# Three whole heads and a pad of eight in each block of 128 features

## The chip, the cores and the metric

The kernel runs on one core of a Trainium2 chip. Its time is device microseconds of one execution; the kernel before takes 280.08 us, the median of three runs (280.01 to 280.14). The engines are named as the profile names them: PE is TensorE (PEld its weight loads), DVE is VectorE, ACT is ScalarE, POOL is GpSimd, SP is the engine that issues nearly all DMAs.

## The reference

A transformer block with linear attention over 2048 positions of width 640, 32 heads of 20, and a gated feed-forward of width 1536. All inputs are bf16.

```python
def _A_ref(x, wqkv, w_phi, wo):
    B, S, D = x.shape
    H = 32; Dh = D // H
    qkv = (lambda x, *d: x.transpose(*d))((x @ wqkv).reshape(B, S, 3, H, Dh), 2, 0, 3, 1, 4)
    q, k, v = qkv[0], qkv[1], qkv[2]
    pq = jnp.einsum("bhsd,hdf->bhsf", q, w_phi)
    pk = jnp.einsum("bhsd,hdf->bhsf", k, w_phi)
    phi_q = jnp.concatenate([_softmax(pq, axis=-1), _softmax(-pq, axis=-1)], axis=-1)
    phi_k = jnp.concatenate([_softmax(pk, axis=-1), _softmax(-pk, axis=-1)], axis=-1)
    kv = jnp.einsum("bhsf,bhsd->bhfd", phi_k, v)
    z  = jnp.einsum("bhsf->bhf", phi_k)
    num = jnp.einsum("bhqf,bhfd->bhqd", phi_q, kv)
    den = jnp.einsum("bhqf,bhf->bhq", phi_q, z)[..., None] + 1e-6
    o = num / den
    return (lambda x, *d: x.transpose(*d))(o, 0, 2, 1, 3).reshape(B, S, D) @ wo

h = x + _A_ref(_layernorm(x), A_wqkv, A_w_phi, A_wo)
h2 = h + ((n @ w_gate) * (n @ w_up)) @ w_down      # n = _layernorm(h)
```

Each head has 40 features: the softmax of 20 scores and the softmax of the same scores negated. The 32 heads make 1280 features.

## The kernel before, in words

The positions are 16 tiles of 128, in four batches of four. The weights of the scores are folded once (`w_phi` into `wqkv`), so that a tile's scores are one projection of 640 columns. Work is cut into named units, each with instructions on several engines:

- `k`t, `v`t, `q`t (`keys`, `values`, `queries`): the projection of tile t on PE, ten matmuls of 320 columns (five blocks of the width by two halves, one half to each bank of a PSUM pair). For keys and queries DVE takes the largest score of the row (L818) and scales it (L821), and ACT writes two exponentials (L825), of the scores and of their negatives, in place side by side per head.
- `K`t: DVE adds up each of the 64 groups of 20 (L836) and takes the reciprocals (L838), POOL multiplies the features by them (L839). `Q`t: DVE adds up the groups (L858), and POOL scales the second half of each head against the first (L864, L869), since numerator and denominator share the rest. Then SP issues two DMA transposes (L471) of 640 features each, which bring the queries' features onto partitions.
- `A`t (`kv_mm`): for the key tiles t and t+1, K^T V. The 1280 features are ten blocks of 128 (`NQ`). A block starts and ends inside a head, so it touches four heads (`SL`), and its matmul streams the values of four heads and their column of ones: 4 x 21 = 84 columns (`KVW`). The features are the weights, the values the moving operand. Two units per pair of tiles, five blocks each, accumulate in the two banks of one PSUM pair that is held from the first A unit to `Aout`.
- `Aout` (`kv_out`): DVE brings K^T V to SBUF, multiplied by a mask (`Gk`) that keeps only a feature's own head (L905), and the column of sums likewise (L908), for each bank.
- `n`t (`num`): phi_q KV of tile t, ten matmuls of 84 columns; neighbouring blocks add into the head that they share. DVE divides (L939, L941). The result is turned (by SP, or by PE for tiles 0 and 1).
- `h`t (`watt`): the output projection, the residual and the sums of the second norm. `f`b.ft.j (`fu`): gate and up of one block of 128 hidden features for a batch, `d`t and `e`t (`fd`): down and the output.

All matmuls go through one helper, so they stand at L570, and are told apart by their tiles: `ps<-vaug,phik` with 84 columns is the A units, `ps<-KVsb,phiqT` the n units, `ps<-Wp,xT` the projections.

The order of the units on each engine is written out by hand in `ORDER` (L58 to L107): each engine runs its list strictly in that order. `Prog.place` assigns the buffers along those lists, among them the four PSUM pairs (`p_ps`) that all units share and the three buffers of query features (`p_eq`), and waits on semaphores follow from the reads and writes that each unit names.

Of the kernel before, what the change touches and what calls it, by code (L numbers as in the profile page):

```python
# [11 lines left out]
P = 128  # L12
# [18 lines left out]
NQ = 2 * NC  # L31
HQ = [P * c // DF for c in range(NQ)]
SL = 4
KVW = SL * E21

# [37 lines left out]
    "DVE":  # L73
# [12 lines left out]
    "ACT":  # L86
# [291 lines left out]
def _build(ctx, nc, A_x, A_wqkv, A_w_phi, A_wo, B_w_gate, B_w_up, B_w_down, out):  # L378
# [68 lines left out]
    p_ps, p_eq, p_ob, p_outb, p_t32, p_gate, p_junk = Pool(4), Pool(3), Pool(2), Pool(2), Pool(2), Pool(2), Pool(2)  # L447
# [13 lines left out]
    R_const, R_xone, R_tab = Reg(), Reg(), Reg()  # L461
# [86 lines left out]
    for a in range(NC):
        lo, hi = CH[a]
        n = hi - lo + 1  # L550

        def phi_op(e, a=a, lo=lo, hi=hi, n=n):
            return e.tensor_tensor(out=Phi[:, a, 0:DH * n].rearrange("p (h f) -> p h f", f=DH),
                                   in0=Wrows[:, a, :].unsqueeze(1).to_broadcast([P, n, DH]),
                                   in1=G[:, a, lo:hi + 1].unsqueeze(2).to_broadcast([P, n, DH]), op=ALU.mult)
# [260 lines left out]
    def softexp(v, t, i, dst, regs_, use=()):
        mx = lambda: PS[v.i][:, 1, MXC:MXC + 1]
        g.op("DVE", lambda e: e.tensor_reduce(out=mx(), in_=PS[v.i][:, :, 0:HALF], axis=AX.XY, op=ALU.max,  # L818
# [4 lines left out]
        for s in range(2):  # L823
            sc = rs if s == 0 else nrs
            g.op("ACT", lambda e, s=s, sc=sc: e.activation(  # L825
                out=signed(dst(), s), in_=PS[v.i][:, :, 0:HALF].rearrange("p b (h f) -> p b h f", f=DH), func=ACT.Exp,
                bias=nb[:, i:i + 1], scale=sc[:, t:t + 1]), rd=v.R + [R_nb[i], R_rs[t], R_nrs[t]], wr=[regs_[s]], use=[v] + list(use),
                t=0.775, lat=0.92)
# [287 lines left out]
```

## Time and profile before

| what | value |
|---|---|
| median of the runs | 280.08 us (280.01 to 280.14) |
| profiled execution, first to last instruction | 278.3 us (no other time of it is listed) |
| PE busy | 274.1 us, 99% |
| DVE busy | 165.3 us, 59% |
| ACT busy | 134.5 us, 48% |
| POOL busy | 106.2 us, 38% |
| 84-column matmuls of the A units | 160, busy 6.7 us |
| 84-column matmuls of the n units | 160, busy 8.7 us |

The page gives busy time over the whole span and, in 40 slices of some 7 us each, in tenths. "Idle before" in a group is time in which the engine stood still ahead of that group, with what ended most of it. A matmul's listed duration has its way through the array in it and overlaps the next one's; what a matmul costs in a row of matmuls is the distance from start to start, which the timeline's stretches give: (length less one listed duration) / (count less one).

### The profile page before, as it was taken

The page shows a single profiled execution, that of the slowest core. Times are in us where ns is not written, and L with a number is a line of the kernel's source. Part 1 is how long each engine was busy: PE and PEld are TensorE (multiplying, and loading weights), DVE is VectorE, ACT ScalarE, POOL GpSimd, SP SyncE. Part 2 cuts the span into 40 slices and gives each one's busy share as a digit, 9 for nine tenths or more (in the row PEclk, how much of TensorE's full clock was granted, in tenths as well). Part 3 has the DMA queues.
Part 4 walks back from the last instruction along what each step waited for, and adds up shares of the span by engine and source line. Part 5 has one row for each costly group of instructions (what it writes and reads, how often), then busy time and mean ns, then how long its engine had stood idle before and what let it go on. Part 6 is the DMA issues. An engine that isn't in the chain of part 4 may idle for free.

```text
span 278.3 us, 5485 instructions
## 1 busy us (share of the span) xinstructions
PE 274.1 (99%) x2239; PEld 186.9 (67%) x2239; DVE 165.3 (59%) x314; ACT 134.5 (48%) x229; POOL 106.2 (38%) x150
## 2 busy tenths in 40 slices
PE   8999999999999999999999999999999999999995
PEld 8877777777878888877656555776464444447773
DVE  1999999999999876588545845313251222324011
ACT  3478999899666465421764413113244314340132
POOL 5438889899732240061320903142100000250252
PEclk9999999999999999999999999999999999999999
DMA  7988886008864617969643031544312000000112
GB/s 196 277 148 185 126 271 251 0 2 236 167 82 110 97 27 155 336 100 198 88 111 82 24 71 27 123 89 97 94 30 20 0 0 2 0 24 24 49 47 71
DMA packets 65193, 28.06 MB, mean 101 GB/s; under 512 B 55697, under 2 KB 63889, under 8 KB 65169
## 3 DMA queue, kind: packets, MB, share of 16 engines
q1 hardware_dynamic: 64240, 27.37, 43.8%
q10 hardware_dynamic: 928, 0.35, 0.5%
q8 instruction: 17, 0.28, 0.4%
q14 instruction: 8, 0.06, 0.1%
HBM read 11.82 MB, written 2.62 MB: 52 GB/s over the span
## 4 chain that ended last, share of the span: by engine, by line
PE 95%; DMA 2%; SPq 1%; DVE 1%; issue 0%
PE ps L570 95%; DMA Wp<-in_A_wqkv_dram 2%; SPq L471 1%; PE ps L482 0%; DVE outb L1022 0%; SPq L467 0%; DVE KVsb L905 0%; DVE KVsb L908 0%; DVE nb L821 0%
## 5 line engine op out<-in xcount | busy, mean ns | idle before, releaser
L570 PE MATMUL ps<-phik,Wgu 128*128 128x512 bf16 (+1 forms) x600 | 107.5, 336 | 0.0
L570 PEld LDWEIGHTS ps<-phik,Wgu 128*128 128x128 bf16 x600 | 58.2, 98 | 43.6 <-DVE phik L981 1.8
L570 PE MATMUL ps<-Wp,xT 128*128 128x320 bf16 x480 | 69.0, 299 | 0.0
L981 DVE TENSOR_TENSOR phik<-ps,gate 128x512 bf16<-128x512 f32 (+1 forms) x60 | 33.9, 577 | 55.3 <-PE ps L570 50.1
L570 PE MATMUL ps<-vaug,phik 128*128 128x320 bf16 (+3 forms) x544 | 60.0, 270 | 0.0
L979 ACT ACTIVATE gate<-ps 128x512 bf16<-128x512 f32 (+1 forms) x60 | 29.8, 510 | 59.7 <-PE ps L570 40.8
L570 PEld LDWEIGHTS ps<-Wp,xT 128*128 128x128 bf16 x480 | 45.9, 98 | 17.6 <-DVE phik L981 0.2
L570 PEld LDWEIGHTS ps<-vaug,phik 128*128 128x128 bf16 x544 | 43.7, 97 | 15.7
L839 POOL TENSOR_TENSOR phik<-phik,Rk 128x1280 bf16<-128x1280 bf16 x16 | 37.5, 2356 | 5.1 <-DVE Rk L838 4.8
L997 POOL TENSOR_TENSOR outb<-t,x_all 128x640 bf16<-128x640 f32 x12 | 16.8, 1397 | 56.9 <-ACT t L994 49.6
L994 ACT ACTIVATE t<-ps,mh,rs 128x640 f32<-128x640 f32 x12 | 10.6, 882 | 37.1 <-PE ps L570 37.1
L818 DVE TENSOR_REDUCE ps<-ps 128x1 f32<-128x640 f32 x32 | 26.3, 824 | 1.6 <-PE ps L570 1.2
L858 DVE TENSOR_REDUCE Sq<-eq 128x64 f32<-128x1280 bf16 x16 | 23.5, 1471 | 3.5 <-ACT eq L825 3.5
L825 ACT ACTIVATE eq<-ps,nb,rs 128x640 bf16<-128x640 f32 x16 | 14.2, 885 | 20.3 <-DVE nb L821 11.7
L836 DVE TENSOR_REDUCE Ssum<-phik 128x64 f32<-128x1280 bf16 x16 | 23.5, 1474 | 0.0
L964 POOL TENSOR_SCALAR vpe<-shc 128x1 f32<-128x1 f32 x16 | 3.0, 190 | 52.7 <-ACT junk L563 51.7
L869 POOL TENSOR_TENSOR eq<-eq,rq 128x640 bf16<-128x640 bf16 x16 | 20.2, 1270 | 0.5
L864 POOL TENSOR_TENSOR rq<-Sq,rq 128x32 f32<-128x32 f32 x16 | 4.0, 254 | 41.5 <-DVE rq L863 41.5
L563 ACT ACTIVATE junk<-x_all 128x640 bf16<-128x640 bf16 x20 | 14.6, 732 | 4.4 <-DVE x_all L958 4.4
L825 ACT ACTIVATE phik<-ps,nb,rs 128x640 bf16<-128x640 f32 x16 | 14.2, 889 | 2.4 <-DVE nb L821 2.4
L825 ACT ACTIVATE phik<-ps,nb,nrs 128x640 bf16<-128x640 f32 x16 | 14.3, 894 | 0.0
L825 ACT ACTIVATE eq<-ps,nb,nrs 128x640 bf16<-128x640 f32 x16 | 14.2, 885 | 0.0
(86 smaller groups left out, 235.8 us busy)
## 6 DMA issues: line engine op xcount, KB each, us to landing
x_all<-in_A_x_dram SPq DMA_DIRECT2D x4, 640.0 KB, 5.2
out_dram<-outb SPq DMA_DIRECT2D x15, 160.0 KB, 1.8
Wgu<-in_B_w_gate_dram SPq DMA_DIRECT2D x1, 1920.0 KB, 11.1
Wgu<-in_B_w_up_dram SPq DMA_DIRECT2D x1, 1920.0 KB, 9.1
vaug<-in_B_w_down_dram SPq DMA_DIRECT2D x1, 1920.0 KB, 8.3
Wp<-in_A_wqkv_dram SPq DMA_DIRECT2D x1, 800.0 KB, 4.9
phiqT<-in_A_wqkv_dram SPq DMA_DIRECT2D x1, 800.0 KB, 6.5
Wo<-in_A_wo_dram SPq DMA_DIRECT2D x1, 800.0 KB, 6.8
```

The source lines that it names most:

```text
L563: g.op("ACT", lambda e: e.activation(out=junk[:, v.i, :], in_=in_, func=func, accum_out=acc), rd=rd, wr=wr, use=[v], t=0.73, lat=0.97)
L570: ins = e.matmul(o_, lhsT=l_, rhs=r_, start=s_, stop=p_, skip_group_check=True)
L818: g.op("DVE", lambda e: e.tensor_reduce(out=mx(), in_=PS[v.i][:, :, 0:HALF], axis=AX.XY, op=ALU.max, apply_absolute_value=True, negate=Tru ...
L825: g.op("ACT", lambda e, s=s, sc=sc: e.activation(out=signed(dst(), s), in_=PS[v.i][:, :, 0:HALF].rearrange("p b (h f) -> p b h f", f=DH), ...
L836: g.op("DVE", lambda e: e.tensor_reduce(out=Ssum[:, vs.i, :], in_=x, axis=AX.X, op=ALU.add), rd=R_phik[t], wr=vs.R, use=[vs], t=1.39, lat=1.5)
L839: g.op("POOL", lambda e: e.tensor_tensor(out=x, in0=x, in1=Rk[:, vr.i, :].unsqueeze(2).to_broadcast([P, 2 * H, DH]), op=ALU.mult), rd=vr.R ...
L858: g.op("DVE", lambda e: e.tensor_reduce(out=Sq[:, vs.i, :], in_=eq[:, b.i, :].rearrange("p (g f) -> p g f", f=DH), axis=AX.X, op=ALU.add), ...
L869: return e.tensor_tensor(out=x, in0=x, in1=rq[:, vr.i, :].unsqueeze(2).to_broadcast([P, H, DH]), op=ALU.mult)
L979: g.op("ACT", lambda e: e.activation(out=gate[:, vg.i, 0:P * n], in_=PS[v.i][:, 0, 0:P * n], func=ACT.Copy), rd=[v.R[0]], wr=vg.R, use=[v, ...
L981: g.op("DVE", lambda e: e.tensor_tensor(out=hhT[:, hb, ft, sl], in0=PS[v.i][:, 1, 0:P * n], in1=gate[:, vg.i, 0:P * n], op=ALU.mult), rd=[ ...
L994: g.op("ACT", lambda e: e.activation(out=t32[:, v3.i, :].rearrange("p (b n) -> p b n", b=2), in_=PS[v.i][:, :, 0:HALF], func=ACT.Identity, ...
L997: g.op("POOL", lambda e: e.tensor_tensor(out=outb[:, vo.i, :], in0=t32[:, v3.i, :], in1=x_all[:, t, :], op=ALU.add), rd=v3.R + [R_h[t]], w ...
```

## The change

A block of 128 features now holds exactly three heads (`HW`), 120 features, and a pad of eight in front (`PADW`). There are 11 blocks (`NQ`), the last with two heads and an empty slot. A block touches three heads, so the matmuls of the A and n units stream 63 columns; the last block's in the n units 42.

- The key features keep their dense layout behind a pad of eight zeros at the very front. A block of weights begins eight features ahead of its first head, so its pad rows are the last features of the head before. The mask `Gk` sets their rows of K^T V to zero. The last block begins one head early.
- The query features get the padded layout: `eq` has 1408 columns instead of 1280. The pads and the empty slot are set once to one (unit `pad` on POOL). Each of a query's two exponentials is written by two ACT instructions, one for ten blocks (600 scores) and one for the last (40). To let the first read run on across the two PSUM banks, the query projection now puts 300 columns at the end of the first bank and 340 at the start of the second, in matmuls of these widths. The sums, reciprocals and products run over 66 groups instead of 64.
- The transposes take five and six blocks instead of five and five; the blocks are split 5 and 6 (15 and 17 heads) in K^T V, its eviction and the n units too.
- `KVsb` lies where `Phi` was; the scratch of the sums of squares (`junk`) has one buffer instead of two.
- `ORDER` is new for all engines behind the first loads. Up to the first n unit each engine but POOL and ACT has the same units as before in its list. SP issues the second feed-forward weight (`lu`) directly behind the first (`lg`), ahead of the transposes of queries 0 and 1.

```diff
+HW = 3
+NQ = 11
+PADW = P - HW * DF
+KVW = HW * E21
+WB = ((0, 5), (5, NQ))
+HB = 5 * HW
...
 ORDER = {
     "PE":
...
-        "k12 v9 v12 v15 v14 k14 k15 A0 A2 A4 v8 q2 q3 A6 v10 A0 A2 A8 q5 A10 A4 A12 A6 A8 A10 A14 A12 A14 n1 n0 n0 n1 q7 "
+        "v14 k14 v12 k15 A0 A2 A0 q2 A2 A4 A4 q3 A6 v10 A6 q5 A8 A10 A8 A12 A10 A12 A14 A14 n0 n1 n0 n1 q7 n1 q4 n0 h1 h0 n2 q6 "
...
     "SP":
-        "in in in in in in in lwq t4 lT7 lT4 t2 lT5 lT6 t3 t1 t0 lx3 lT10 lT15 lT9 lT11 lT8 lT13 lT14 lT12 lx0 lwo lg Q0 "
-        "Q0 lu Q1 Q1 Q2 Q2 Q3 Q3 Q5 Q5 n2 n3 Q7 Q7 h2 Q4 h3 Q4 Q6 Q6 Q8 ld n7 n5 lx1 n4 n6 Q8 Q9 h5 lx2 Q9 h4 n8 h7 h6 "
+        "in in in in in in in lwq t4 lT7 lT4 t2 lT5 lT6 t3 t1 t0 lx3 lT10 lT15 lT9 lT11 lT8 lT13 lT14 lT12 lx0 lwo lg lu Q1 Q0 "
+        "Q1 Q0 Q2 Q2 Q3 Q3 Q5 Q5 n2 n3 Q7 Q7 h2 h3 Q4 Q4 ld Q6 n5 Q6 n7 lx1 Q8 n4 Q8 lx2 n6 n8 h7 Q9 Q9 h5 h6 h4 Q10 Q10 Q12 "
...
-    BK = sb([P, 2 * NT * D], BF16, "phik")
+    BK = sb([P, PADW + 2 * NT * D], BF16, "phik")
-    eq = sb([P, 3, 2 * D], BF16, "eq")
-    junk = sb([P, 2, D], BF16, "junk")
+    eq = sb([P, 3, NQ * P], BF16, "eq")
+    junk = sb([P, 1, D], BF16, "junk")
...
+    U("pad")
+    pool_op(lambda e: e.memset(eq[:, :, :].rearrange("p b (w n) -> p b w n", n=P)[:, :, :, 0:PADW], 1.0), 0.4, wr=[R_pad])
+    pool_op(lambda e: e.memset(eq[:, :, (NQ - 1) * P + PADW:(NQ - 1) * P + PADW + DF], 1.0), 0.2, app=[R_pad])
+    pool_op(lambda e: e.memset(BK[:, 0:PADW], 0.0), 0.1, wr=[R_pad0])
...
         for s in range(2):
             sc = rs if s == 0 else nrs
-            g.op("ACT", lambda e, s=s, sc=sc: e.activation(
-                out=signed(dst(), s), in_=PS[v.i][:, :, 0:HALF].rearrange("p b (h f) -> p b h f", f=DH), func=ACT.Exp,
...
+            for k, (to, of, n) in enumerate(pieces):
+                g.op("ACT", lambda e, s=s, sc=sc, to=to, of=of: e.activation(
+                    out=to(s), in_=of(), func=ACT.Exp, bias=nb[:, i:i + 1], scale=sc[:, t:t + 1]),
...
     def queries(t, after=()):
         U("q%d" % t)
-        v = proj(t, 0, after)
+        v = Buf(p_ps, 2)
+        cut = HB * DH
+        g.op("PE", lambda e: mms(e, [(flat(v)[:, 512 - cut:512] if bk == 0 else flat(v)[:, 512:512 + D - cut], xT[:, t, c, 0:P],
+                                      Wp[:, c, cut * bk:cut + (D - cut) * bk], c == 0, c == NC - 1)
+                                     for c in range(NC) for bk in range(2)]),
...
+        softexp(v, t, NT + t, lambda: score(0, D),
+                [(lambda s: feat()[:, 0:NQ - 1, :].rearrange("p w (h s f) -> p s w h f", s=2, f=DH)[:, s],
+                  lambda: score(0, 2 * cut).rearrange("p (w h f) -> p w h f", h=HW, f=DH), 2 * cut),
+                 (lambda s: feat()[:, NQ - 1, DF:].rearrange("p (h s f) -> p s h f", s=2, f=DH)[:, s],
+                  lambda: score(2 * cut, D).rearrange("p (h f) -> p h f", f=DH), D - 2 * cut)], b.R, [b])
...
-        for k in range(2):
-            transpose(lambda k=k: phiqT[:, bb, NC * k:NC * (k + 1), P * tt:P * (tt + 1)], lambda k=k: eq[:, b.i, D * k:D * (k + 1)],
+        for k, (w0, w1) in enumerate(WB):
+            transpose(lambda w0=w0, w1=w1: phiqT[:, bb, w0:w1, P * tt:P * (tt + 1)], lambda w0=w0, w1=w1: eq[:, b.i, P * w0:P * w1],
...
     def kv_mm(t0, t1):
...
-                for c in range(NC * k, NC * (k + 1)):
-                    lo = HQ[c]
-                    col = KVW * (c - NC * k)
+                for w in range(w0, w1):
+                    h0 = min(HW * w, H - HW)
                     for t in range(t0, t1):
-                        o_ = (t * H + lo) * E21
-                        lst.append((PS[v.i][:, k, col:col + KVW], phik[:, t, P * c:P * (c + 1)], BV[:, o_:o_ + KVW], first, False))
+                        k0, o_ = 2 * D * t + HW * DF * w, (t * H + h0) * E21
+                        if w == NQ - 1:
+                            k0 -= DF
+                        lst.append((PS[v.i][:, k, KVW * (w - w0):KVW * (w - w0 + 1)], BK[:, k0:k0 + P], BV[:, o_:o_ + KVW], first, False))
...
     def num(t):
...
+                for bk in range(b0, b1):
+                    for w in range(*WB[bk]):
+                        k0 = KVW * w + (E21 if w == NQ - 1 else 0)
+                        o_ = base + KVW * w
+                        n = KVW * (w + 1) - k0
+                        lst.append((flat(v)[:, o_:o_ + n], phiqT[:, bb, w, P * tt:P * (tt + 1)], KVsb[:, k0:k0 + n], w == WB[bk][0], False))
```

More of the change, by code (lines that the diff above doesn't have):

```diff
@@ L30 @@
 DF = 2 * DH
[L31 to L34, printed above, removed]
+HW = 3
[4 more added lines that the diff above has]
+HB = 5 * HW
 WOW = D + 4
@@ L425, in _build @@
     Rk = sb([P, 2, 2 * H], FP32, "Rk")
-    Sq = sb([P, 2, 2 * H], FP32, "Sq")
-    rq = sb([P, 2, H], FP32, "rq")
+    Sq = sb([P, 2, 2 * HW * NQ], FP32, "Sq")
+    rq = sb([P, 2, HW * NQ], FP32, "rq")
     rden = sb([P, 2, H], FP32, "rden")
-    phik = BK[:, :].rearrange("p (t n) -> p t n", t=NT)
+    Phi = PK[:, :].rearrange("p (a n) -> p a n", a=NC)
+    KVsb = PK[:, 0:NQ * KVW]
+    phik = BK[:, PADW:PADW + 2 * NT * D].rearrange("p (t n) -> p t n", t=NT)
     pq = phiqT[:, :, :, :].rearrange("p b c n -> p (b c n)")
@@ L851, in queries, with score, feat @@
         U("q%d" % t)
-        v = proj(t, 0, after)
+        v = Buf(p_ps, 2)
[3 more added lines that the diff above has]
+                                     for c in range(NC) for bk in range(2)]),
+             rd=[R_xT[t]] + R_Wp[0], wr=v.R, use=[v], t=1.3575, lat=1.5075, after=after)
         bb, tt = (t // 4) % 2, t % 4
         b = Buf(p_eq, 2)
-        softexp(v, t, NT + t, lambda: eq[:, b.i, :], b.R, [b])
+        def score(lo, hi):
+            return flat(v)[:, 512 - cut + lo:512 - cut + hi]
+        def feat():
+            return eq[:, b.i, :].rearrange("p (w n) -> p w n", n=P)[:, :, PADW:P]
+        softexp(v, t, NT + t, lambda: score(0, D),
[3 more added lines that the diff above has]
+                  lambda: score(2 * cut, D).rearrange("p (h f) -> p h f", f=DH), D - 2 * cut)], b.R, [b])
         vs, vr = Buf(p_Sq), Buf(p_rq)
         U("Q%d" % t)
-        g.op("DVE", lambda e: e.tensor_reduce(out=Sq[:, vs.i, :], in_=eq[:, b.i, :].rearrange("p (g f) -> p g f", f=DH),
-                                              axis=AX.X, op=ALU.add), rd=b.R, wr=vs.R, use=[b, vs], t=1.4, lat=1.5)
+        g.op("DVE", lambda e: e.tensor_reduce(out=Sq[:, vs.i, :].rearrange("p (w g) -> p w g", w=NQ),
+                                              in_=feat().rearrange("p w (g f) -> p w g f", f=DH),
+                                              axis=AX.X, op=ALU.add), rd=b.R + [R_pad], wr=vs.R, use=[b, vs], t=1.44, lat=1.54)
         def sums(k):
@@ L899, in kv_out, with psv @@
         v = KVBUF
-        for k in range(2):
-            dst = KVsb[:, NC * KVW * k:NC * KVW * (k + 1)].rearrange("p (c h e) -> p c h e", c=NC, e=E21)
-            def psv(k=k):
-                return PS[v.i][:, k, 0:NC * KVW].rearrange("p (c h e) -> p c h e", c=NC, e=E21)
-            g.op("DVE", lambda e, psv=psv, dst=dst: e.tensor_tensor(
-                out=dst[:, :, :, 0:DH], in0=psv()[:, :, :, 0:DH], in1=Gk[:, :, :].unsqueeze(3).to_broadcast([P, NC, SL, DH]), op=ALU.mult),
-                rd=[v.R[k], R_Gk], app=[R_KV[k]], use=[v], t=0.5, lat=0.6)
-            g.op("DVE", lambda e, psv=psv, dst=dst: e.scalar_tensor_tensor(
-                out=dst[:, :, :, DH], in0=psv()[:, :, :, DH], scalar=0.5 * EPS_DEN, in1=Gk[:, :, :], op0=ALU.add, op1=ALU.mult),
+        for k, (w0, w1) in enumerate(WB):
+            n = HW * (w1 - w0)
+            dst = KVsb[:, KVW * w0:KVW * w1].rearrange("p (h e) -> p h e", e=E21)
+            gk = Gk[:, :, :].rearrange("p w h -> p (w h)")[:, 0:n]
+            def psv(k=k, n=n):
+                return PS[v.i][:, k, 0:E21 * n].rearrange("p (h e) -> p h e", e=E21)
+            g.op("DVE", lambda e, psv=psv, dst=dst, gk=gk, n=n: e.tensor_tensor(
+                out=dst[:, :, 0:DH], in0=psv()[:, :, 0:DH], in1=gk.unsqueeze(2).to_broadcast([P, n, DH]), op=ALU.mult),
+                rd=[v.R[k], R_Gk], app=[R_KV[k]], use=[v], t=0.07 + 0.0213 * n, lat=0.18 + 0.0213 * n)
+            g.op("DVE", lambda e, psv=psv, dst=dst, gk=gk: e.scalar_tensor_tensor(
+                out=dst[:, :, DH], in0=psv()[:, :, DH], scalar=0.5 * EPS_DEN, in1=gk, op0=ALU.add, op1=ALU.mult),
                 rd=[v.R[k], R_Gk], app=[R_KV[k]], use=[v], t=0.09, lat=0.25)
@@ L922, in f @@
                 lst = []
-                for c in range(NC * b0, NC * b1):
-                    bk = c // NC
-                    col = E21 * (HQ[c] - HH2 * bk)
-                    lst.append((PS[v.i][:, bk, col:col + KVW], phiqT[:, bb, c, P * tt:P * (tt + 1)], KVsb[:, KVW * c:KVW * (c + 1)],
-                                c % NC == 0, False))
+                for bk in range(b0, b1):
[4 more added lines that the diff above has]
+                        lst.append((flat(v)[:, o_:o_ + n], phiqT[:, bb, w, P * tt:P * (tt + 1)], KVsb[:, k0:k0 + n], w == WB[bk][0], False))
@@ L928, in f @@
                 return mms(e, lst)
-            g.op("PE", f, rd=R_KV[b0:b1] + [R_phiqT[bb][k][tt] for k in range(b0, b1)], wr=v.R[b0:b1], use=[v],
-                 t=0.19 * (b1 - b0), lat=0.15 + 0.19 * (b1 - b0))
+            n = sum(WB[bk][1] - WB[bk][0] for bk in range(b0, b1)) * 0.0288 + 0.015
+            g.op("PE", f, rd=R_KV[b0:b1] + [R_phiqT[bb][k][tt] for k in range(b0, b1)], wr=v.R[b0:b1], use=[v], t=n, lat=0.15 + n)
         for b0, b1 in halves:
-            n = b1 - b0
-            def pv(b0=b0, b1=b1):
-                return PS[v.i][:, b0:b1, 0:E21 * HH2].rearrange("p b (h e) -> p b h e", e=E21)
@@ L937, in rd_ @@
-            def rd_(b0=b0, b1=b1):
-                return rden[:, vr.i, HH2 * b0:HH2 * b1].rearrange("p (b h) -> p b h", b=b1 - b0)
-            g.op("DVE", lambda e, pv=pv, rd_=rd_: e.reciprocal(out=rd_(), in_=pv()[:, :, :, DH]), rd=v.R[b0:b1], wr=vr.R[b0:b1],
-                 use=[v, vr], t=0.06 + 0.105 * n, lat=0.17 + 0.105 * n)
-            g.op("DVE", lambda e, pv=pv, rd_=rd_, b0=b0, b1=b1: e.tensor_tensor(
-                out=ob[:, vo.i, HALF * b0:HALF * b1].rearrange("p (b h d) -> p b h d", b=b1 - b0, d=DH), in0=pv()[:, :, :, 0:DH],
-                in1=rd_().unsqueeze(3).to_broadcast([P, b1 - b0, HH2, DH]), op=ALU.mult),
-                rd=v.R[b0:b1] + vr.R[b0:b1], wr=vo.R[b0:b1], use=[v, vr, vo], t=0.07 + 0.3375 * n, lat=0.185 + 0.3375 * n)
+            h0, h1 = (0, HB)[b0], (0, HB, H)[b1]
@@ new lines, in num, with pv @@
+            n = h1 - h0
+            def pv(h0=h0, h1=h1):
+                return flat(v)[:, base + E21 * h0:base + E21 * h1].rearrange("p (h e) -> p h e", e=E21)
+            g.op("DVE", lambda e, pv=pv, h0=h0, h1=h1: e.reciprocal(out=rden[:, vr.i, h0:h1], in_=pv()[:, :, DH]), rd=v.R[b0:b1],
+                 wr=vr.R[b0:b1], use=[v, vr], t=0.06 + 0.00656 * n, lat=0.17 + 0.00656 * n)
+            g.op("DVE", lambda e, pv=pv, h0=h0, h1=h1, n=n: e.tensor_tensor(
+                out=ob[:, vo.i, DH * h0:DH * h1].rearrange("p (h d) -> p h d", d=DH), in0=pv()[:, :, 0:DH],
+                in1=rden[:, vr.i, h0:h1].unsqueeze(2).to_broadcast([P, n, DH]), op=ALU.mult),
+                rd=v.R[b0:b1] + vr.R[b0:b1], wr=vo.R[b0:b1], use=[v, vr, vo], t=0.07 + 0.0211 * n, lat=0.185 + 0.0211 * n)
@@ L1067, in _build @@
         kv_mm(t, t + 2)
+    g.alias(R_KV, R_Phi)
     kv_out()
```

49 lines of the change are left out of this document (28 added, 21 removed), and 79 rows, old and new, of the table ORDER.

## The prediction

> **What bounds the kernel now.** I read the page's head and slices first, then the chain that ended last in order of time, then busy time by stage, and last the groups and the timeline around the two matmul groups that the change rewrites.
>
> ```profile
> span 278.3 us, 5485 instructions
> PE 274.1 (99%) x2239; PEld 186.9 (67%) x2239; DVE 165.3 (59%) x314; ACT 134.5 (48%) x229; POOL 106.2 (38%) x150
> PE   8999999999999999999999999999999999999995
> DVE  1999999999999876588545845313251222324011
> PEclk9999999999999999999999999999999999999999
> ...
> 37.36 37.00 PE ps L570 x406
> ...
> 74.38 0.58 DVE KVsb L905
> 74.96 0.15 DVE KVsb L908
> ...
> 84.13 190.70 PE ps L570 x1322
> ```
>
> TensorE is busy from end to end at the full granted clock, and the chain of waits lies on it except for 0.73 us of VectorE's KV eviction at 74.4. From 84.13 to 274.83 it is one unbroken run of matmuls: there, a matmul made shorter shortens the kernel, unless another engine then comes late. The slices show who: VectorE stands at 9 tenths up to about 90 us. The stages say how full it is (columns: window, length, then busy time of PE, PEld, DVE, ACT, POOL with counts).
>
> ```profile
> 10.00:73.60 63.60, 63.58 (x671) 48.80 (x670) 62.26 (x116) 55.27 (x87) 52.24 (x55) 1.00 0.69 162
> 73.60:75.60 2.00, 1.74 (x41) 1.47 (x38) 1.94 (x8) 0.43 (x1) 0.42 (x2) 1.00 0.42 80
> 75.60:84.10 8.50, 8.45 (x84) 6.27 (x81) 8.33 (x20) 5.84 (x9) 3.20 (x5) 1.00 0.63 87
> 84.10:95.00 10.90, 10.87 (x99) 9.07 (x100) 10.35 (x20) 6.47 (x13) 3.04 (x4) 1.00 0.57 94
> 95.00:126.00 31.00, 31.00 (x295) 25.98 (x294) 22.24 (x47) 14.00 (x33) 8.49 (x16) 1.00 0.67 152
> ```
>
> From 10 to 73.6 VectorE is idle for 1.34 us only (63.60 less 62.26), from 75.6 to 84.1 for 0.17. So up to 84 two engines are full at once, and time taken from TensorE alone is worth at most what VectorE can follow. After 95 VectorE is free a quarter of the time.
>
> The profiled execution's span is 278.3; the runs' median is 280.08, 1.8 more, which I take as unchanged beside the span. All sums are made on the span. From no change I can tell about 0.2%, 0.56 us.
>
> **The change, part by part.** The rows that price a matmul:
>
> ```profile
> 62.44 4.24 PE L570 MATMUL ps<-Wp,xT 128*128 128x320 bf16 x30
> 70.75 3.59 PE L570 MATMUL ps<-vaug,phik 128*128 128x84 bf16 x90
> 40.41 0.64 PE L570 MATMUL ps<-ones,xT 128*128 128x1 bf16 x20
> 84.13 0.55 PE L570 MATMUL ps<-KVsb,phiqT 128*128 128x84 bf16 x10
> 84.51 1.52 PE L570 MATMUL ps<-Wp,xT 128*128 128x320 bf16 x10
> L570 PE MATMUL ps<-Wp,xT 128*128 128x320 bf16 x480 | 69.0, 299 | 0.0
> L570 PE MATMUL ps<-KVsb,phiqT 128*128 128x84 bf16 x160 | 8.7, 201 | 0.3 <-DVE nb L821 0.2
> L570 PE MATMUL ps<-vaug,phik 128*128 128x84 bf16 x160 | 6.7, 200 | 0.0
> L570 PE MATMUL ps<-ones,xT 128*128 128x1 bf16 x20 | 0.6, 163 | 0.0
> ```
>
> Each of these has a weight load of its own. Start to start: 320 columns (4.24 - 0.299)/29 = 136 ns; 84 columns (3.59 - 0.200)/89 = 38.1 ns; one column (0.64 - 0.163)/19 = 25 ns, the floor of a pair of load and matmul. The line through the first two is 0.415 ns a column and 3.3 ns fixed, so 63 columns come to 29.4 ns, above the floor, and the 42 of the last block stay at 25 ns.
>
> - K^T V (A units): 160 x 38.1 = 6.10 us become 176 x 29.4 = 5.17: 0.93 less TensorE time.
> - phi_q KV (n units): ten took 0.38 (84.13 to 84.51), eleven take 10 x 29.4 + 25 = 319 ns: 0.06 less, for 16 tiles 0.98.
> - Query projections, 300 and 340 columns for two of 320: equal.
>
> So 1.9 us leave TensorE. What of it reaches the end, stage by stage:
>
> ```profile
> 71.96 1.43 DVE L858 TENSOR_REDUCE Sq<-eq 128x64 f32<-128x1280 bf16 x1
> 73.62 0.58 DVE L905 TENSOR_TENSOR KVsb<-ps,Gk 128x400 bf16<-128x400 f32 x1 [0.24 <-PE ps L570]
> 74.12 0.23 DVE L908 SCALAR_TENSOR_TENSOR KVsb<-ps,Gk 128x20 bf16<-128x20 f32 x1
> 75.17 0.56 PE L570 MATMUL ps<-KVsb,phiqT 128*128 128x84 bf16 x10 [0.20 <-DVE nb L821]
> 83.16 0.82 DVE L941 TENSOR_TENSOR ob<-ps,rden 128x640 bf16<-128x640 f32 x1
> 70.06 2.36 POOL L839 TENSOR_TENSOR phik<-phik,Rk 128x1280 bf16<-128x1280 bf16 x1
> ```
>
> A stage. In both orders VectorE has the same list of work ahead of the KV eviction, the sums of the fourth query last, and it ended these at 73.39 and waited 0.24 for TensorE. That 0.24 is all an earlier A stage can take from it. Against it stand four query sums over 1320 instead of 1280 elements (1471 ns by its group, about 1.04 ns an element: 0.05 each, with the reciprocal 33 wide) = 0.2 later. The A unit of the last key tile was reached behind sixty of the ninety matmuls, at 73.04; 88 and 66 shorter ones around the last projection, instead of 70 and 60, bring it to 72.6. POOL's product of that tile ended at 72.42, so it stays just behind. The eviction moves 660 elements instead of 800: 0.13 shorter. The second eviction so ends 0.24 - 0.2 + 0.13 = 0.17 earlier. TensorE, busy for 1.74 of the 2.00 us there, waits 0.76 longer: most of the 0.93 is lost in front of the first n units.
>
> 75 to 84. n3 started at 84.13, just behind VectorE's output of n2 (83.16 + 0.82 = 83.98), with VectorE full from 75 on. It inherits the 0.17, less 0.05 for one more query sum: 0.12 earlier.
>
> From n3 on TensorE sets the end, and thirteen n units are left: 13 x 0.06 = 0.80.
>
> Sum: 278.3 - 0.12 - 0.80 = 277.4, which is 279.2 for the runs.
>
> What I cost at nothing, and its cover:
>
> ```profile
> 66.95 0.88 ACT L825 ACTIVATE eq<-ps,nb,rs 128x640 bf16<-128x640 f32 x1
> 67.72 0.89 ACT L825 ACTIVATE eq<-ps,nb,nrs 128x640 bf16<-128x640 f32 x1
> L979 ACT ACTIVATE gate<-ps 128x512 bf16<-128x512 f32 x36 | 20.8, 596 | 45.1 <-PE ps L570 32.4 <-DVE phik L981 12.6
> L979 ACT ACTIVATE gate<-ps 128x256 bf16<-128x256 f32 x24 | 9.0, 382 | 14.5 <-PE ps L570 8.4 <-DVE phik L981 5.0 <-DVE rq L863 1.1
> ACT eq L825 <- DMA phiqT<-eq: 2.5, 2, 1.3
> L471 SPq DMA_TRANSPOSE phiqT<-eq x28: 1199/1277/1967, 74.0 to 180.8; - x28
> L869 POOL TENSOR_TENSOR eq<-eq,rq 128x640 bf16<-128x640 bf16 x16 | 20.2, 1270 | 0.5
> POOL Phi L553 <- DMA Wrows<-in_A_w_phi_dram: 2.1, 1, 2.1
> POOL outb L690 <- DVE nmean L688: 0.8, 1, 0.8
> ```
>
> Exponentials: a query has four ScalarE instructions instead of two. The two gate shapes give (596 - 382)/256 = 0.84 ns an element and 168 ns fixed; two exponentials start 0.77 apart while one lasts 0.88, so 0.11 of the fixed part overlaps. One more instruction costs between 0.06 and 0.17, a query 0.12 to 0.34; I take 0.2, nearer the start-to-start row. ScalarE has idle time in every stage above (8 us up to 73.6, a third of 75.6 to 84.1), so this is no bound; but a query's PSUM pair is held that much longer, and only four pairs exist. Left out of the sum; it is the second rival. [...]
>
> Transposes: six blocks instead of five in every second one. By 1.28 us for five SP spends 0.25 more per query, and the landing shifts alike. Two queries already wait for these (2.5 us in all), on ScalarE. With the cover gone, 0.25 each.
>
> The 16 POOL products grow by 20 elements (1270 ns for 640: 0.04 each), with POOL 38% busy. The three pad memsets are under a microsecond by POOL's other memsets and stand in its early waits (2.1 and 0.8). The larger gate-weight load now leaves ahead of the first query transposes instead of between them; the n units were waiting for VectorE by then, so nothing. One scratch buffer instead of two concerns ScalarE alone. The order behind the first loads is new on all engines; its lists up to n3 are the same work, and I price it at nothing with the next-to-last rival as its risk.
>
> **The rivals.**
>
> All of it arrives. If the new order also takes out VectorE's 1.34 us of idle time before 73.6, the A stage gives its 0.93 too: 280.08 - 1.9 = 278.2. For it: that idle time is there. Against it: VectorE's list ahead of the eviction is unchanged in content and 0.2 longer. 0.15.
>
> Given back in the query stages. 16 queries hold PSUM 0.12 to 0.34 longer and transposes land 0.25 later. Break-even is at 0.92/16 = 0.06 us of TensorE wait per query. If half of them cost 0.1, 0.8 is lost: 280.0, no change; if the new order brings waits of 0.1 to all, 280.8. For it: TensorE's tasks follow their buffers' release closely, as n3 does with 0.15. Against it: ScalarE's and VectorE's idle time after 95. 0.25.
>
> Slower: shifted weights. The key blocks used as weights began at multiples of 256 bytes; now they begin 240 bytes apart, behind a pad. No row shows weights at such addresses. From below the price is nothing (29.4 ns a pair); from above the nearest row is the pair of 128 columns, five of which took 0.44, so (0.44 - 0.219)/4 = 55 ns:
>
> ```profile
> 76.92 0.44 PE L482 MATMUL ps<-ident,ob 128*128 128x128 bf16 x5
> L482 PE MATMUL ps<-ident,ob 128*128 128x128 bf16 x10 | 0.9, 219 | 0.0
> ```
>
> At 55 ns for all 176 the A stage takes 9.7 us, 3.6 more than before, less the 0.98 of the n units: 282.7; for every second block alone 280.4. It decides from (5.17 + 0.81 + 0.92)/176 = 39 ns a pair on, since 0.81 of the A stage's gain is lost anyway. Against it: the value operand, at uneven addresses already, shows no cost in the 38 ns. I take nothing. 0.10.
>
> Weight loads set the pace. The pair costs what its load costs, however few columns stream: then 32 more pairs at an unchanged 38.1 ns add 1.2 us, 281.3. [...] 0.02.
>
> **How the numbers follow.** The sum as it stands has 0.48 and by itself 278.8 to 279.6: the A stage's share between 0 and 0.5 and a wait or two. The range takes in the full gain below and the given-back case above, 278.0 to 280.8, and leaves out the dearer half of shifted weights and pace. Faster by over 0.2%, below 279.5: 0.48 and 0.15 and a little of the second rival less the edge, 0.64. Within 0.2%: most of the second rival, 0.20. Slower: the dear end of it and the last two, 0.16.
>
> **What would show it.** In the profile after: 63-column matmuls at about 29 ns start to start in the A units, all blocks alike; n units of eleven in 0.32; the first n units still behind VectorE's KV eviction with a TensorE gap of over 1 us there; the last unbroken TensorE run starting near 84.0 and lasting 189.9. It is wrong if the A pairs take 39 ns or more, if the eviction comes 0.5 earlier or later than here, or if waits for ScalarE's query exponentials or for transposes appear in the chain behind 84 us.

## The result, and the profile after

The changed kernel takes 280.74 us (median of 12 runs, 280.47 to 280.98), the kernel before in the same comparison 280.07 (279.93 to 280.51). The ratio is 1.0022 with a 95% interval of 1.0013 to 1.003: a small loss, where 279.2 us and a gain was forecast. The profiled execution's span grew from 278.3 to 278.7 us.

The head of the page after, three of its 40-slice rows, and the pieces of the chain that ended last, in order of time (start, length, what):

```profile
span 278.7 us, 5593 instructions
...
PE 272.0 (98%) x2257; PEld 183.8 (66%) x2271; DVE 167.8 (60%) x314; ACT 142.7 (51%) x261; POOL 108.1 (39%) x153
...
PE   7999999999899999999999999999999999999995
...
DVE  2999999989999887684587463523342212241012
...
PEclk9999999999999999999999999999999999999999
```

```profile
43.11 2.05 ACT eq L836 x4
...
53.88 0.66 issue
54.55 2.15 ACT eq L836 x4
...
56.74 15.15 PE ps L577 x178
...
76.00 4.37 DMA phiqT<-eq
...
81.38 1.42 ACT eq L836 x3
85.29 52.97 PE ps L577 x495
```

TensorE has less to do (272.0 us busy instead of 274.1) and the granted clock is still 1.00, so the lost time is waiting. Before, the chain lay on TensorE from 9 us to the last output, except for the KV eviction; now ScalarE's query exponentials (`eq L836`) stand in it at 43, 54 and 81 us, and a transfer of query features at 76. The long run of matmuls that ends the kernel starts about one microsecond later. (The trace lacks 14 matmul records, 2257 against 2271 weight loads. The short breaks in that run behind 138 us go with these: the three variants below whose traces lack none, with loops swapped or short exponentials left out in places, have the same run without a break.)

The same stages as before (window, length, busy time of PE, PEld, DVE, ACT, POOL):

```profile
10.00:73.60 63.60, 63.24 (x678) 47.29 (x676) 61.39 (x115) 56.72 (x91) 51.87 (x53) 1.00 0.69 164
73.60:75.60 2.00, 1.23 (x40) 1.12 (x36) 2.00 (x6) 0.44 (x3) 1.13 (x1) 1.00 0.00 0
75.60:84.10 8.50, 8.20 (x85) 5.67 (x82) 8.18 (x22) 7.61 (x16) 3.36 (x5) 1.00 0.71 95
```

Up to 73.6 us VectorE is busy for 61.39 us instead of 62.26. Its list up to there is no shorter; its idle time grew by 0.87 us. The timeline of VectorE shows nearly all of that in one place, and ScalarE's timeline shows why (start, length, operation, in brackets the idle time ahead and what ended it):

```profile
55.28 0.55 DVE L852 RECIPROCAL Rk<-Ssum 128x64 f32<-128x64 f32 x1
56.72 1.53 DVE L888 TENSOR_REDUCE Sq<-eq 128x66 f32<-128x1320 bf16 x1 [0.89 <-ACT eq L836]
...
75.05 0.52 DVE L940 TENSOR_TENSOR Phi<-ps,Gk 128x360 bf16<-128x360 f32 x1
75.49 0.23 DVE L943 SCALAR_TENSOR_TENSOR Phi<-ps,Gk 128x18 bf16<-128x18 f32 x1
```

```profile
43.01 1.13 ACT L836 ACTIVATE eq<-ps,nb,rs 128x600 bf16<-128x600 f32 x2
44.01 1.14 ACT L836 ACTIVATE eq<-ps,nb,nrs 128x600 bf16<-128x600 f32 x2
...
53.85 0.80 ACT L859 ACTIVATE vaug<-ps,rs 128x640 bf16<-128x640 f32 x1 [0.65 <-PE ps L577]
54.55 1.12 ACT L836 ACTIVATE eq<-ps,nb,rs 128x600 bf16<-128x600 f32 x2
55.55 1.14 ACT L836 ACTIVATE eq<-ps,nb,nrs 128x600 bf16<-128x600 f32 x2
```

One sign of a query (a long instruction and a short one) takes 44.01 - 43.01 = 1.00 us from start to start. Before it took 67.72 - 66.95 = 0.77, by the rows that the prediction shows. So a query costs ScalarE 0.46 us more. Query 0 leaves ScalarE late, and TensorE's weight loads, which come first of a projection, wait for the PSUM pair that it held and for the one behind it (the last row is used further down):

```profile
45.20 1.20 PEld L577 LDWEIGHTS ps<-Wp,xT 128*128 128x128 bf16 x10 [0.47 <-ACT eq L836]
46.75 5.29 PEld L577 LDWEIGHTS ps<-Wp,xT 128*128 128x128 bf16 x40 [0.35 <-ACT phik L836]
...
82.84 0.40 PEld L577 LDWEIGHTS ps<-Phi,phiqT 128*128 128x128 bf16 x11 [0.42 <-ACT eq L836]
```

So the next projections come late, and with them the value tile at 53.85, behind which query 1's exponentials stand in ScalarE's list. (ScalarE's wait of 0.65 us ahead of this value tile is not itself the price: it is 0.65 and 0.69 in two variants below that have no wait of VectorE there.) Query 1's exponentials start at 54.55 and take 0.46 longer in their turn, and VectorE, with nothing else allowed in its list, waits 0.89 for their sum. That is about twice the 0.46, as if the lateness of query 0 and query 1's own added up. The second KV eviction ends at 75.49 + 0.23 = 75.72 instead of 75.11, and the first unit behind which TensorE is never late again, n3, starts at 85.14:

```profile
75.24 1.06 PE L577 MATMUL ps<-Phi,phiqT 128*128 128x63 bf16 x22 [0.77 <-DVE Phi L943]
...
78.19 1.54 PE L577 MATMUL ps<-Wp,xT 128*128 128x300 bf16 x10 [0.16 <-ACT eq L836]
...
85.14 0.49 PE L577 MATMUL ps<-Phi,phiqT 128*128 128x63 bf16 x11
```

That is 1.01 later than before's 84.13. Of this 0.61 came with the eviction. The other 0.40 was lost behind it, from its end to n3 (9.42 us instead of 9.02), where TensorE waits twice more for ScalarE: 0.16 for query 5's exponentials ahead of the projection at 78.19, and about 0.26 for query 7's ahead of the unit n2 at 82.84, whose weight loads wait (n2 starts 3.00 us behind the output projections' start, before it was 2.74). Behind n3 the thirteen shorter n units give back 0.53: the stretch to TensorE's last matmul takes 190.17 us (to 275.31) instead of 190.70, and 278.3 + 1.01 - 0.53 = 278.8, against 278.7 measured.

### The profile page after: what moved, and what is told of

It is laid out like the page before. It is cut to its first block, busy times and chain, and to the rows that moved or that the text cites. A ratio compares the mean times of both kernels' runs of the same rounds, so it can differ in the third digit from the quotient of the medians.

```text
span 278.7 us, 5593 instructions
## 1 busy us (share of the span) xinstructions
PE 272.0 (98%) x2257; PEld 183.8 (66%) x2271; DVE 167.8 (60%) x314; ACT 142.7 (51%) x261; POOL 108.1 (39%) x153
## 4 chain that ended last, share of the span: by engine, by line
PE 86%; ACT 5%; DMA 3%; SPq 2%; issue 1%; DVE 1%; POOL 1%; ACTq 0%
PE ps L577 86%; ACT eq L836 2%; DMA Wp<-in_A_wqkv_dram 2%; ACT phik L836 2%; DMA phiqT<-eq 2%; SPq L473 1%; POOL eq L900 0%; ACT Wp L773 0%; DVE outb L1058 0%; ACT junk L570 0%; DVE ps L828 0%; SPq L469 0%; ACT vaug L859 0%; PE ps L484 0%; DVE rq L894 0%
## 5 line engine op out<-in xcount | busy, mean ns | idle before, releaser
L577 PE MATMUL ps<-Wp,xT 128*128 128x320 bf16 (+1 forms) x480 | 70.0, 299 | 0.5 <-ACT eq L836 0.4
L577 PE MATMUL ps<-vaug,phik 128*128 128x320 bf16 (+3 forms) x559 | 59.3, 265 | 0.1
L888 DVE TENSOR_REDUCE Sq<-eq 128x66 f32<-128x1320 bf16 x16 | 24.3, 1520 | 8.3 <-ACT eq L836 8.1
L895 POOL TENSOR_TENSOR rq<-Sq,rq 128x33 f32<-128x33 f32 x16 | 4.1, 258 | 55.8 <-DVE rq L894 43.5
L836 ACT ACTIVATE eq<-ps,nb,rs 128x600 bf16<-128x600 f32 (+1 forms) x32 | 18.1, 616 | 7.6 <-DVE nb L831 5.9
L900 POOL TENSOR_TENSOR eq<-eq,rq 128x660 bf16<-128x660 bf16 x16 | 20.9, 1308 | 1.0
L836 ACT ACTIVATE eq<-ps,nb,nrs 128x600 bf16<-128x600 f32 (+1 forms) x32 | 18.6, 625 | 0.0
L836 ACT ACTIVATE phik<-ps,nb,rs 128x640 bf16<-128x640 f32 x16 | 14.2, 890 | 2.1 <-DVE nb L831 2.1
L1051 DVE SCALAR_TENSOR_TENSOR outb<-ps,rs,t 128x640 bf16<-128x640 f32 x3 | 2.7, 884 | 20.4 <-PE ps L577 20.4
L994 DVE SCALAR_TENSOR_TENSOR x_all<-ps,mh,x_all 128x640 bf16<-128x640 f32 x16 | 13.9, 870 | 0.7
```

What stands on the lines that cost most here:

```text
L577: ins = e.matmul(o_, lhsT=l_, rhs=r_, start=s_, stop=p_, skip_group_check=True)
L836: g.op("ACT", lambda e, s=s, sc=sc, to=to, of=of: e.activation(out=to(s), in_=of(), func=ACT.Exp, bias=nb[:, i:i + 1], scale=sc[:, t:t + 1 ...
L888: g.op("DVE", lambda e: e.tensor_reduce(out=Sq[:, vs.i, :].rearrange("p (w g) -> p w g", w=NQ), in_=feat().rearrange("p w (g f) -> p w g f ...
L900: return e.tensor_tensor(out=x, in0=x, in1=rq[:, vr.i, :].rearrange("p (w h) -> p w h", h=HW).unsqueeze(3).to_broadcast([P, NQ, HW, DH]), ...
L994: g.op("DVE", lambda e: e.scalar_tensor_tensor(out=xv, in0=PS[v.i][:, :, 0:HALF], scalar=mh[:, t:t + 1], in1=xv, op0=ALU.subtract, op1=ALU ...
```

## The experiments

Eight variants were run. Each ratio below is to the kernel before, measured beside it on the same chip.

**The short exponentials left out.** Heads 30 and 31 of the queries are not computed; ScalarE's list loses the entries, and the unit `pad` sets these features to one.

```diff
-                  lambda: score(0, 2 * cut).rearrange("p (w h f) -> p w h f", h=HW, f=DH), 2 * cut),
-                 (lambda s: feat()[:, NQ - 1, DF:].rearrange("p (h s f) -> p s h f", s=2, f=DH)[:, s],
-                  lambda: score(2 * cut, D).rearrange("p (h f) -> p h f", f=DH), D - 2 * cut)], b.R, [b])
+                  lambda: score(0, 2 * cut).rearrange("p (w h f) -> p w h f", h=HW, f=DH), 2 * cut)], b.R, [b])
```

> The changed kernel without the two 40-score exponentials of each query (heads 30 and 31 of the queries keep the value one, so their part of the output is left out); the list of ScalarE loses these entries, nothing else is moved. Theory 'price': a further ScalarE instruction costs 0.23 us, 0.46 per query (two signs take 2.14 us in the trace after, 1.66 before), and in the full K stage that makes VectorE wait 0.89 us for query 1. Then this gives back the 0.5 us of TensorE waits at 44 to 57 us, VectorE's wait at 56 us and the wait ahead of the projection of query 4, and the time is 279.3 (279.0 to 279.6). Theory 'order': the list of ScalarE has query 1 behind the values of tile 11, and that alone makes VectorE wait; then the wait stays and the time is 280.5.

Measured: 279.29 us, ratio 0.9971 (0.9959 to 0.9983). The groups of ScalarE in the changed kernel, by shape (busy us, mean ns of one), show what was taken away:

```profile
L836 ACT ACTIVATE eq<-ps,nb,rs 128x600 bf16<-128x600 f32 x16 | 13.6, 850 | 7.6 <-DVE nb L831 5.9 <-DMA phiqT<-eq 1.8
L836 ACT ACTIVATE eq<-ps,nb,nrs 128x40 bf16<-128x40 f32 x16 | 6.3, 395 | 0.0
L836 ACT ACTIVATE eq<-ps,nb,rs 128x40 bf16<-128x40 f32 x16 | 6.1, 382 | 0.0
```

Forty scores take 0.39 us in this list, 600 take 0.85. Without the short ones the kernel is as fast as it was forecast; 1.0022 - 0.9971 = 0.51% of the time, 1.4 us, is theirs. This does not yet say whether the second instruction costs, or only that 40 scores fewer are computed; the fifth run tells that.

**The value tile behind query 1.** Only the order changes: the eviction that ScalarE waited for goes behind query 1's exponentials.

```diff
 ORDER = {
     "ACT":
...
-        "k5 k5 v1 s12 k10 k10 q0 q0 q0 q0 k11 k11 v6 wo0 v13 k8 k8 k9 k9 v15 v11 q1 q1 q1 q1 k12 v9 k12 v8 wo4 k13 k13 v14 k14 "
+        "k5 k5 v1 s12 k10 k10 q0 q0 q0 q0 k11 k11 v6 wo0 v13 k8 k8 k9 k9 v15 q1 q1 q1 q1 v11 k12 v9 k12 v8 wo4 k13 k13 v14 k14 "
```

> The changed kernel with one move in ScalarE's list: the values of tile 11 come behind the four exponentials of query 1 instead of ahead of them. Theory 'price': VectorE's 0.89 us of wait at 56 us goes, but the query costs what it did, the key and value evictions behind it come later, and only a part comes back: 280.2 to 280.6. Theory 'order': the wait and all that follows from it goes, 279.7 or less.

Measured: 280.39 us, ratio 1.0012 (1.0004 to 1.0021). VectorE's timeline has a wait of the same size in another place:

```profile
61.06 0.83 DVE L828 TENSOR_REDUCE ps<-ps 128x1 f32<-128x640 f32 x1 [0.86 <-PE ps L577]
```

Query 1 is in time: its sum starts at 55.87 instead of 56.72. But the value tile's eviction starts at 55.23 instead of 53.85, so the tile holds its PSUM pair longer, and the scores that VectorE reads at 61.06 come late from TensorE. The lateness moved, and the time stays within the range of 'price'. That position in the order alone is not the cause.

**The kernel before with each query exponential cut in two.** Nothing else of the change, and the order of before; the cut is at the bank, 320 scores each.

```diff
+            for bk in range(2):
+                g.op("ACT", lambda e, s=s, sc=sc, bk=bk: e.activation(
+                    out=signed(dst(), s)[:, bk], in_=PS[v.i][:, bk, 0:HALF].rearrange("p (h f) -> p h f", f=DH), func=ACT.Exp,
```

> The kernel before, with each exponential of a query cut in two, one for each PSUM bank (16 heads each): 32 further ScalarE instructions and nothing else changed, in its old order. Theory 'price': 0.46 us per query on a ScalarE that is nearly full in the K stage, TensorE waits in several places: 280.7 to 281.5. Theory 'order': the old order bears it, 280.1 to 280.3.

Measured: 282.26 us, ratio 1.0077 (1.0064 to 1.0089), 2.2 us slower than before and more than the expectation's upper end. The timelines of ScalarE and VectorE:

```profile
43.15 1.13 ACT L831 ACTIVATE eq<-ps,nb,rs 128x320 bf16<-128x320 f32 x2
44.15 1.14 ACT L831 ACTIVATE eq<-ps,nb,nrs 128x320 bf16<-128x320 f32 x2
```

```profile
51.19 0.83 DVE L817 TENSOR_REDUCE ps<-ps 128x1 f32<-128x640 f32 x1 [0.45 <-PE ps L569]
...
61.08 0.83 DVE L817 TENSOR_REDUCE ps<-ps 128x1 f32<-128x640 f32 x1 [0.50 <-PE ps L569]
...
73.60 1.49 DVE L864 TENSOR_REDUCE Sq<-eq 128x64 f32<-128x1280 bf16 x1 [0.62 <-ACT eq L831]
```

A sign takes 1.00 us again, so the price does not hang on the short instruction, the pads or the crossing of banks: it is that of a second instruction. It alone makes a kernel slower, with waits of VectorE in three places.

**The changed operations in the order of before.** `ORDER` has the lists of the kernel before, with each query four times instead of twice on ACT and the three `pad` units added on POOL. A part of TensorE's list:

```diff
 ORDER = {
     "PE":
...
-        "v14 k14 v12 k15 A0 A2 A0 q2 A2 A4 A4 q3 A6 v10 A6 q5 A8 A10 A8 A12 A10 A12 A14 A14 n0 n1 n0 n1 q7 n1 q4 n0 h1 h0 n2 q6 "
+        "v15 v14 k14 k15 A0 A2 A4 v8 q2 q3 A6 v10 A0 A2 A8 q5 A10 A4 A12 A6 A8 A10 A14 A12 A14 n1 n0 n0 n1 q7 n1 q4 n0 h1 h0 n2 "
```

> The changed kernel's operations in the old order of all five engines (the query entries of ScalarE doubled, the three pads put into POOL's early waits). Theory 'price': the price is paid in the old order too, and the old order was not laid out for it: 280.3 to 281. Theory 'order': what is lost is lost by the new order, so the old one keeps the matmuls' gain: 279.4 or less.

Measured: 283.22 us, ratio 1.0109 (1.0096 to 1.0123), 2.2 us above the expectation's upper end. With these operations the new order is worth 1.0109 - 1.0022 = 0.87%, 2.4 us, so going back to the old one recovers nothing. Why it costs even more than the split in the kernel before was not traced.

**One exponential per sign, computed in full.** The empty slot moves from the last block to the first, so that the 32 heads and the slot are one run of 660 scores. The first query matmul fills the slot's 20 columns with scores that nothing reads.

```diff
+HB = 5 * HW - 1
...
-                        k0, o_ = 2 * D * t + HW * DF * w, (t * H + h0) * E21
+                        k0, o_ = 2 * D * t + HW * DF * w, (t * H + HW * w - 1) * E21
...
-                [(lambda s: feat()[:, 0:NQ - 1, :].rearrange("p w (h s f) -> p s w h f", s=2, f=DH)[:, s],
-                  lambda: score(0, 2 * cut).rearrange("p (w h f) -> p w h f", h=HW, f=DH), 2 * cut),
-                 (lambda s: feat()[:, NQ - 1, DF:].rearrange("p (h s f) -> p s h f", s=2, f=DH)[:, s],
-                  lambda: score(2 * cut, D).rearrange("p (h f) -> p h f", f=DH), D - 2 * cut)], b.R, [b])
+                [(lambda s: feat().rearrange("p w (h s f) -> p s w h f", s=2, f=DH)[:, s],
+                  lambda: score(-DH, D).rearrange("p (w h f) -> p w h f", h=HW, f=DH), D + DH)], b.R, [b])
```

> The changed kernel computed in full, with the missing head put first: block w holds heads 3w-1, 3w and 3w+1, block 0 the two heads 0 and 1 behind an empty slot, so each sign of a query is one exponential over 660 scores (20 of the empty slot, whose numbers nothing reads) and ScalarE has two instructions per query again, in the order of the run without the tail. The first query matmul covers 300 columns instead of 280, about 8 ns more per query; ScalarE reads 60 more scores per sign than there, about 0.06 us. 'The second instruction is the price': one sign takes 0.90 to 0.93 us of ScalarE where the two instructions took 1.00 us, VectorE's wait of 0.89 us ahead of the query sum near 56 us falls below 0.5 us, and the time is 279.3 to 279.7 us, against 280.7 of the changed kernel. 'The number of scores that a query exponentiates is the price' (the run without the tail left 40 of 640 out, and was fast for that): one sign stays at 1.00 us and the time at 280.3 us or more.

Measured: 279.35 us, ratio 0.9959 (0.9945 to 0.9972): faster than both kernels. ScalarE's timeline and the end of the chain:

```profile
43.52 0.90 ACT L835 ACTIVATE eq<-ps,nb,rs 128x660 bf16<-128x660 f32 x1
44.30 0.91 ACT L835 ACTIVATE eq<-ps,nb,nrs 128x660 bf16<-128x660 f32 x1
```

```profile
74.42 0.39 DVE Phi L946
74.82 0.15 DVE Phi L949
...
83.16 0.83 DVE ob L983
83.99 0.14 issue
84.13 190.16 PE ps L576 x1335
```

More scores than in any other variant, and a sign takes 0.78 us (the 0.90 of the expectation is the length of one instruction, not the distance). VectorE's wait is gone, the chain is back on VectorE and TensorE alone, and n3 starts at 84.13, where it started before. TensorE's two later waits for query exponentials are gone too, but for some 0.04 us (n2 starts 2.78 behind the output projections). It is the number of instructions, not of scores.

The clock times of the traces are a little apart from the start: the first weight load, on which every chain lies, lands at 9.32 us before, at 9.24 in the changed kernel, and here at 9.66. Counted from it, n3 comes 0.34 earlier here than before.

**The two loops of a K^T V unit swapped.** This is on another question: the n units came out at 0.34 us, not 0.32, because in the trace after their 63-column matmuls are 32 ns apart and those of the A units 29 (medians; the means are 31.6 and 29.5).

```diff
-                for w in range(w0, w1):
-                    h0 = min(HW * w, H - HW)
-                    for t in range(t0, t1):
+                for t in range(t0, t1):
+                    for w in range(w0, w1):
+                        h0 = min(HW * w, H - HW)
```

> The changed kernel with the two loops of a K^T V unit swapped: its matmuls go through all blocks of one tile and then of the other, so that each adds into another 63 columns than the one before it, as the matmuls of phi_q KV do; sums and counts are the same. 'Another column range costs': the pairs of K^T V go from 29 ns to the 32 ns of phi_q KV, and the 22 units take 0.15 to 0.6 us longer. 'It is something else of phi_q KV' (the weights, or the end of a unit): the pairs stay at 29 ns.

Measured in one profiled run (280.87 us): the stretch of 88 matmuls in TensorE's timeline of the changed kernel, and then of this one:

```profile
71.72 2.76 PE L577 MATMUL ps<-vaug,phik 128*128 128x63 bf16 x88
```

```profile
72.01 2.88 PE L577 MATMUL ps<-vaug,phik 128*128 128x63 bf16 x88
```

With 193 ns as the listed length of one, the 88 went from (2.76 - 0.193)/87 = 29.5 to (2.88 - 0.193)/87 = 30.9 ns apart, and all 176 are busy for 6.2 us instead of 6.0. So a wider distance is nothing peculiar to phi_q KV: the same matmuls of K^T V go 1.4 ns further apart in another sequence. The expectation named the column range that is written; the swap also changes the sequence of weights and values, so which of these costs the 1.4 ns stays open, and that the n units have their 31.6 ns for the same reason was not shown.

**The short exponentials left out in two places.** First for queries 0 and 1 alone, then for the nine queries behind n3 (tiles 6 and 8 to 15), where the edited condition is `t == 6 or t > 7`.

```diff
-                  lambda: score(2 * cut, D).rearrange("p (h f) -> p h f", f=DH), D - 2 * cut)], b.R, [b])
+                  lambda: score(2 * cut, D).rearrange("p (h f) -> p h f", f=DH), D - 2 * cut)][0:1 if t < 2 else 2], b.R, [b])
```

> The changed kernel with the short exponential over 40 scores left out for tiles 0 and 1 alone (heads 30 and 31 of their queries keep what the buffer holds); four of the 32 short ones. 'The price arrives where VectorE is full': queries 0 and 1 are exponentiated between 43 and 57 us, where VectorE has no idle time, and their lateness is VectorE's wait of 0.89 us at 56; without it the time falls by 0.5 to 0.9 us, to 279.8 to 280.3. 'The price is paid evenly by all queries': an eighth of the 1.45 us that all short ones cost comes back, 0.18, and the time is 280.5 to 280.6.

> The changed kernel with the short exponential left out for the nine queries behind the unit n3 (tiles 6 and 8 to 15), 18 of the 32 short ones. 'The price arrives where VectorE is full': these queries run behind 85 us, where TensorE waited for nothing; the time stays at 280.5 to 280.9. 'The price is paid evenly by all queries': nine sixteenths of 1.45 us come back, 0.8, and the time is 279.8 to 280.1.

Measured: without those of queries 0 and 1, 279.73 us, ratio 0.9982 (0.9973 to 0.9991), a little better than expected; without those of nine late queries, 280.70 us, ratio 1.0018 (1.0009 to 1.0027), no change. Four short instructions of 32 hold 1.0022 - 0.9982 = 0.40 of the 0.51%; eighteen others hold nothing that can be measured. In the first variant VectorE's wait is gone, and the eviction and n3 come 0.8 earlier than in the changed kernel, as these rows of ScalarE (queries of 600 scores alone), VectorE and TensorE show:

```profile
43.15 0.85 ACT L836 ACTIVATE eq<-ps,nb,rs 128x600 bf16<-128x600 f32 x1
43.88 0.85 ACT L836 ACTIVATE eq<-ps,nb,nrs 128x600 bf16<-128x600 f32 x1
```

```profile
74.24 0.52 DVE L940 TENSOR_TENSOR Phi<-ps,Gk 128x360 bf16<-128x360 f32 x1
```

```profile
77.37 1.54 PE L577 MATMUL ps<-Wp,xT 128*128 128x300 bf16 x10 [0.16 <-ACT eq L836]
...
84.32 0.49 PE L577 MATMUL ps<-Phi,phiqT 128*128 128x63 bf16 x11
```

TensorE's 0.16 us for ScalarE at 77.37, where short exponentials are still there, remains, and so does the loss ahead of n2, which again starts 3.00 us behind the output projections (82.03 and 79.03).

## Why the prediction was wrong

The step that failed is the one for the exponentials: "a query 0.12 to 0.34; I take 0.2", with "ScalarE has idle time in every stage above, so this is no bound", left out of the sum.

- The size. A query costs 0.46, above the upper end. The distances from start to start of an exponential are 0.27 us for 40 scores, by 1.00 less the 0.73 of 600 (43.15 to 43.88), and 0.50 for 320, 0.77 for 640 and 0.78 for 660: all of them 0.23 us and 0.84 ns a score. The per-score slope was right. The fixed part had been taken from another function, the gate evictions (168 ns), less the 0.11 by which two exponentials overlap. The exponential's own row had it: 0.77 less 640 x 0.84 ns is 0.23.
- The cover. Idle time of ScalarE over a stage did not cover a delay inside it. Up to 84 us VectorE has next to none (before, 1.34 us up to 73.6), and the query's sum waits for ScalarE with VectorE's whole list behind it. The runs without the short instructions put the price there: 0.40 of 0.51% at queries 0 and 1, nothing behind n3. So the second rival came true, at its upper end, but not in the form it was written, "waits of 0.1 to all" queries: it was one wait of 0.89 us of VectorE, which the eviction passes on to n3 (without it both come 0.8 earlier), and some 0.42 us of TensorE waiting for queries 5 and 7. That the loss came out at this rival's 280.8 is in part luck, since its sum was sixteen waits of 0.1.
- The signs. One that the prediction itself named was met: the eviction, forecast for 75.11 - 0.17 = 74.94, ended 0.78 late. The waits for exponentials stood ahead of 84 us and not behind, where it looked for them.
- "Its lists up to n3 are the same work, and I price it at nothing" did no harm that these runs show: in the old order the same operations take 2.4 us more, and the new order with one instruction per sign has no such wait of VectorE.

The other steps. The A pairs at 29.4 ns were right (29.5 in the row of 88), without a block that stands out (the means of the eleven blocks lie between 28.5 and 30.9 ns), so the rival of shifted weights fell, and that of weight loads, with its unchanged 38.1 ns, too. The n unit was to save 0.06 and saves 0.05, as a unit before and one after show, each with the row behind it:

```profile
98.16 0.55 PE L570 MATMUL ps<-KVsb,phiqT 128*128 128x84 bf16 x10
98.55 2.89 PE L570 MATMUL ps<-phik,Wgu 128*128 128x256 bf16 x25
...
97.77 0.50 PE L577 MATMUL ps<-Phi,phiqT 128*128 128x63 bf16 x11
98.11 0.71 PE L577 MATMUL ps<-phik,Wgu 128*128 128x256 bf16 x5
```

That is 0.34 against 0.39, with the pairs at 32 ns (median) where 29.4 was forecast. Thirteen of these make 0.6 instead of 0.80; the whole stretch from n3 on became 0.53 shorter. The loss of the A stage's gain in front of the first n units was right in kind: between 73.6 and 75.6 us TensorE is busy for 1.23 us instead of 1.74, and the first n units wait 0.77 us for the eviction, where over 1 us was forecast. And where the second instruction is gone, the rest of the sum nearly holds: with one exponential per sign the eviction ends at 74.97, 0.14 earlier than before where 0.17 was forecast, n3 starts at 84.13 where 84.0 was, and the time is 0.9959 of before where 0.997 was. Counted from the first weight load the two are 0.48 and 0.34 earlier, so more of the A stage's gain arrived there than the sum allowed.

What stays open: the 0.1% (0.3 us) that is not at queries 0 and 1 was not tried query by query. The traces put it at queries 5 and 7, by TensorE's 0.16 and 0.26 us, which stay when queries 0 and 1 alone are relieved and are all but gone with one exponential per sign; no run relieved these two alone.

## What to carry to other kernels

Price an added instruction by the start-to-start distance of its own kind: the fixed part is that distance less the elements at the slope (here 0.77 us less 640 x 0.84 ns, 0.23 us), and a row of another function can give too little (here 0.168, less 0.11 of overlap). An engine with idle time on average can still delay what waits for it (here ScalarE, busy for 51% of the span, held VectorE up for 0.89 us); follow the longer step to the engine that has none, and look at what is queued behind its wait. When a layout leaves a remainder, put it where one access pattern still covers everything: here the empty slot at the front instead of the end turned a loss of 0.2% into a gain of 0.4%.

## What the runs showed of the hardware

- An exponential that reads PSUM takes 0.23 us plus 0.84 ns a score in a row of such instructions, within a bank (0.27 us for 40 scores, 0.50 for 320) or across two (0.73 for 600, 0.77 for 640, 0.78 for 660).
- Weights that begin every 240 bytes, behind a pad of 16, cost nothing that these rows show: a pair of weight load and matmul with 63 columns takes 29.5 ns in the row of 88, where the line through the rows of before gave 29.4, an estimate.
- The same 63-column matmuls of K^T V were 29.5 ns apart in the row of 88 with tiles in the inner loop, and 30.9 with blocks in it (one trace each).
